# A list-scheduled attention and GeGLU kernel: partial-wave readiness in the scheduler, other pool sizes, one more full matmul asked for per three narrow waves, other POOL estimates, and a hold-off before tanh

## Chip, cores, metric

One core of one Trainium2 chip. The metric is device time in microseconds (us). Engines: PE (matmul), DVE (vector), ACT (activation), POOL (GpSimd), SP (issues DMAs).

## The reference, cut to what matters

```python
# x: [1, 2048, 512] bf16, 32 heads of 16
g = sigmoid((x * gate_w).sum(-1, keepdims=True))
q, k, v = split(x @ wqkv)
p = softmax(q @ k.T * 16**-0.5)          # per head, 2048 x 2048
a = (p @ v) @ wo
h = gelu_tanh(x @ w_gate) * (x @ w_up)   # 1376 columns
b = h @ w_down
return g * a + (1 - g) * b
```

## The kernel before

The kernel is written as about 7600 tasks. A list scheduler in Python gives each engine a fixed order, working from assumed durations; semaphores then enforce the true dependences. So an assumed duration never changes what an instruction costs. It only changes the order in which each engine's queue is laid down, and the chip runs these queues in order.

The attention is done in "waves" of matmuls on 32 rows. Pass A computes score tiles (128x512) and DVE takes their row maxima; pass B, 80 tiles later, recomputes the transposed tiles with the maximum subtracted, ACT takes exp, and PE multiplies with V ("PV"). A wide wave (D) has two A tiles and two B tiles, a narrow one (S) one of each. Four heads and 512 queries make a unit of 64 tiles; there are 32 units. Between the waves PE does the projections and the feed-forward half.

```python
# one unit, pass A done: its maxima go to PE by way of POOL  ("hand-over")
t_fin = add("dve", ..., name="fin%d" % u, ...)              # L1046 negm
t_hi  = add("pool", 260.0, ..., name="hi%d" % u, ...)       # L1056 CAST
t_lo  = add("pool", 270.0, ..., name="lo%d" % u, ...)       # L1060
#   then PE: QB = ident x QA + Msel x ident                 # L819, L1066
# one unit, PV done: row sums through DRAM, reciprocal, broadcast back
d4 = dma_task("n4_%d" % u, Rb..., 65536 * 4, ...)           # 256 KB, assumed 2.85 us
t_on[u] = add("pool", d_pool(512, 2.4), ..., deps=[d4, t_oe], ...)   # L1122, waits for d4
... # cut
# gelu of one 128x512 tile: ACT copy, three POOL ops, ACT tanh, two POOL ops, POOL times u
t_p3  = add("pool", ..., name="gp3_%d_%d" % (sc, fc), ...)  # L942
t_th2 = add("act", d_act(512) + 30.0, em, name="g_tanh%d_%d" % (sc, fc), deps=[t_p3], uses=[tm_tl])  # L948
... # cut
# dummies: full 128x128x512 matmuls on zeros ahead of a narrow wave, to hold PE's clock
if wna == 1 and plan is not None:
    ndum = plan.get(wi, 0)
# derive_plan, from a FIRST schedule without dummies: any 3 narrow waves in a row
# shall have plan_min full matmuls, at most dummy_max = 2 dummies each
have = sum(r[lo_:i_ + 1]) + sum(d[lo_:i_ + 1])
if have < want:
    d[i_] = min(C["dummy_max"], want - have)
```

## Time and profile before

| | before |
|---|---|
| time, median | 1444.74 us when predicted (4 runs), 1442.74 us over 16 runs |
| pass A (wide reduces) | 15.9 to 1369.9 us of the span |
| tail without reduces | 71.6 us |
| clock at half speed before the last reduce | 119.5 us in 9 stretches |
| full dummies (L1164) | 644 |

From the profile page of the kernel before: busy time of each engine, and the span in 40 slices with PE's granted clock in tenths.

```profile
span 1441.6 us, 22221 instructions
...
PE 1220.1 (85%) x8077; PEld 343.8 (24%) x8077; DVE 1262.8 (88%) x1449; ACT 1234.5 (86%) x2355; POOL 327.9 (23%) x386
...
PEclk9799999999989999998999998799999999799956
```

PE, DVE and ACT are almost equally busy. The 7s and 8s in the clock row are slices that hold stretches at half clock; the 56 at the end is the tail.

The costliest groups of before; columns: line, engine, op, shapes, count, busy us, mean ns, idle us just before and what ended it.

```profile
L1242 ACT ACTIVATE R<-ps 128x512 bf16<-128x512 f32 x2048 | 1098.5, 609 | 119.1 <-PE ps L1194 89.4
L1218 DVE TENSOR_REDUCE pmb<-ps 128x2 f32<-128x1024 f32 x683 | 835.5, 1223 | 87.7 <-PE ps L1194 75.9
...
L1225 DVE TENSOR_REDUCE pmb<-ps 128x1 f32<-128x512 f32 x682 | 463.9, 680 | 16.6 <-PE ps L1194 13.9
...
L1164 PE MATMUL ps<-wrm 128*128 128x512 bf16 x644 | 207.2, 399 | 50.3 <-PE ps L1194 23.2
```

Where DVE never waits, the timeline of before shows a wide and a narrow reduce every 1.81 us (start us, length us):

```profile
604.20 1.21 DVE L1218 TENSOR_REDUCE pmb<-ps 128x2 f32<-128x1024 f32 x1
...
605.37 0.69 DVE L1225 TENSOR_REDUCE pmb<-ps 128x1 f32<-128x512 f32 x1
...
606.00 1.23 DVE L1218 TENSOR_REDUCE pmb<-ps 128x2 f32<-128x1024 f32 x1
```

683 such pairs are 1236 us; pass A takes 1354 us. So about 100 us are lost where DVE waits for PE. Lines of the waits of before (who waited for whom: us, times, longest):

```profile
POOL R L1122 <- DMA Rb<-scr_li: 375.0, 30, 31.9
...
DVE pmb L1218 <- PE ps L1194: 75.9, 155, 2.8
...
POOL tmpb L954 <- ACT tmpb L948: 42.4, 40, 3.3
...
ACT tmpb L948 <- POOL tmpb L942: 4.3, 4, 2.3
```

The last line is four waits and 4.3 us in all.

### The profile page before, as it was taken

To read this page: it belongs to the slowest core of one execution; us is meant where nothing else is said; L and a number is where in the kernel's file an instruction comes from. 1 tells how busy PE (TensorE), PEld (TensorE's weight loads), DVE (VectorE), ACT (ScalarE), POOL (GpSimd) and SP (SyncE) were. 2 spreads that over 40 slices of the span, in tenths; PEclk is the share of its full clock that TensorE was granted. 3 is DMA by queue.
4 is the path that set the end of the run, shared out by engine and by line. 5 is a ranking of instruction groups with operands and counts; after the bars stand their busy time and mean duration, and the time that the engine had idled before them with its cause. 6 is when DMAs were issued, how large, how long until landed. Compare 5 with 4: busy or idle time off the path is not lost.

```text
span 1441.6 us, 22221 instructions
## 1 busy us (share of the span) xinstructions
PE 1220.1 (85%) x8077; PEld 343.8 (24%) x8077; DVE 1262.8 (88%) x1449; ACT 1234.5 (86%) x2355; POOL 327.9 (23%) x386
## 2 busy tenths in 40 slices
PE   9888888888888888889888888888888888888884
PEld 3322222222222222222222222222222222222211
DVE  8889889999987999998998998899998899899900
ACT  3189999999977999888998998799998998799991
POOL 2123431013323330013333410023332400000000
PEclk9799999999989999998999998799999999799956
DMA  6000000000000000000000000000000000000000
GB/s 220 1 15 9 10 2 9 8 10 9 9 9 15 9 9 9 9 9 9 1 9 23 9 9 9 2 9 8 9 9 20 12 9 1 8 9 9 9 8 23
DMA packets 23287, 21.11 MB, mean 15 GB/s; under 512 B 10928, under 2 KB 17424, under 8 KB 23184
## 3 DMA queue, kind: packets, MB, share of 16 engines
q1 hardware_dynamic: 23184, 19.70, 4.2%
q8 instruction: 69, 1.13, 0.3%
q14 instruction: 34, 0.28, 0.1%
HBM read 17.07 MB, written 2.62 MB: 14 GB/s over the span
## 4 chain that ended last, share of the span: by engine, by line
PE 45%; ACT 28%; DVE 20%; issue 4%; DMA 2%; POOL 1%; POOLq 0%
ACT R L1242 22%; PE ps L1177 19%; DVE pmb L1218 14%; PE ps L1164 8%; PE ps L1261 6%; DVE pmb L1225 6%; PE ps L819 5%; PE ps L1194 3%; PE ps L1298 2%; PE ps L992 2%; ACT tmpb L948 1%; DMA Rb<-scr_li 1%; ACT OSb L1099 1%; ACT KT L852 1%; ACT gbb L1002 1%
## 5 line engine op out<-in xcount | busy, mean ns | idle before, releaser
L1242 ACT ACTIVATE R<-ps 128x512 bf16<-128x512 f32 x2048 | 1098.5, 609 | 119.1 <-PE ps L1194 89.4
L1218 DVE TENSOR_REDUCE pmb<-ps 128x2 f32<-128x1024 f32 x683 | 835.5, 1223 | 87.7 <-PE ps L1194 75.9
L1177 PE MATMUL ps<-KT,QAb 32*128 32x512 bf16 x2048 | 540.8, 395 | 134.8 <-DVE pmb L1218 36.2
L1194 PE MATMUL ps<-QBb,KT 32*128 32x512 bf16 x2048 | 543.5, 405 | 6.2 <-PE ps L1261 3.2
L1225 DVE TENSOR_REDUCE pmb<-ps 128x1 f32<-128x512 f32 x682 | 463.9, 680 | 16.6 <-PE ps L1194 13.9
L1177 PEld LDWEIGHTS ps<-KT,QAb 32*128 32x128 bf16 x2048 | 138.8, 91 | 597.8 <-ACT R L1242 379.1
L1164 PE MATMUL ps<-wrm 128*128 128x512 bf16 x644 | 207.2, 399 | 50.3 <-PE ps L1194 23.2
L1261 PE MATMUL ps<-R,Vaug 128*17 128x512 bf16 x2048 | 209.6, 403 | 5.9 <-ACT R L1242 5.6
L1194 PEld LDWEIGHTS ps<-QBb,KT 32*128 32x128 bf16 x2048 | 126.8, 91 | 24.8 <-ACT R L1242 24.0
L1122 POOL TENSOR_TENSOR R<-OSb,Rb 128x512 bf16<-128x512 f32 x32 | 40.5, 1266 | 399.0 <-DMA Rb<-scr_li 375.0
L930 POOL TENSOR_TENSOR tmpb<-gsb 128x512 bf16<-128x512 bf16 (+1 forms) x44 | 45.7, 1038 | 237.6 <-ACT gsb L924 237.6
L1261 PEld LDWEIGHTS ps<-R,Vaug 128*17 128x17 bf16 x2048 | 49.2, 87 | 142.0 <-issue 103.4
L1164 PEld LDWEIGHTS ps<-wrm 128*128 128x128 bf16 x644 | 41.8, 97 | 144.3 <-ACT R L1242 134.8
L1056 POOL CAST Msel<-negm 128x16 bf16<-128x16 f32 x32 | 8.1, 252 | 297.9 <-DVE negm L1046 297.9
L976 POOL TENSOR_TENSOR gsb<-gsb,usb 128x512 bf16<-128x512 bf16 (+1 forms) x44 | 50.7, 1151 | 38.8 <-ACT usb L970 36.7
L819 PE MATMUL ps<-xT,wg 128*128 128x512 bf16 (+1 forms) x176 | 56.1, 388 | 0.8 <-ACT R L1242 0.6
L819 PE MATMUL ps<-xT,wu 128*128 128x512 bf16 (+1 forms) x176 | 55.1, 387 | 1.2 <-ACT R L1242 0.6
L1298 PE MATMUL ps<-R 128*128 128x512 bf16 x128 | 41.5, 452 | 16.5 <-POOL R L1122 13.6
L992 PE MATMUL ps<-wd,gsb 128*128 128x512 bf16 (+1 forms) x176 | 52.5, 383 | 0.0
L942 POOL TENSOR_TENSOR tmpb<-tmpb,gsb 128x512 bf16<-128x512 bf16 (+1 forms) x44 | 50.7, 1152 | 3.6
L960 POOL TENSOR_TENSOR gsb<-gsb,tmpb 128x512 bf16<-128x512 bf16 (+1 forms) x44 | 50.6, 1151 | 3.3
L1112 DVE RECIPROCAL Lci<-Lc 128x16 f32<-128x16 f32 x32 | 7.8, 244 | 46.3 <-DMA Lc<-scr_l 46.3
(62 smaller groups left out, 541.1 us busy)
## 6 DMA issues: line engine op xcount, KB each, us to landing
Rb<-scr_li SPq DMA_DIRECT2D x32, 256.0 KB
R<-in_A_x_dram SPq DMA_DIRECT2D x4, 512.0 KB, 6.4
out_dram<-R SPq DMA_DIRECT2D x16, 128.0 KB, 1.7
wg<-in_B_w_gate_dram SPq DMA_DIRECT2D x1, 1376.0 KB
wu<-in_B_w_up_dram SPq DMA_DIRECT2D x1, 1376.0 KB, 12.1
wd<-in_B_w_down_dram SPq DMA_DIRECT2D x1, 1280.0 KB, 14.5
R<-in_A_wqkv_dram SPq DMA_DIRECT2D x1, 1024.0 KB, 6.2
R<-in_A_wqkv_dram SPq DMA_DIRECT2D x1, 512.0 KB, 9.5
```

Of the source, the lines that this page charges most:

```text
L819: return [e.matmul(psum_ap(tl)[0:m, 0:n], lhsT=lhs_fn(c), rhs=rhs_fn(c), start=(c == 0), stop=(c == nmm - 1))]
L942: return [e.tensor_tensor(out=t_, in0=t_, in1=gsb[0:fr, gs_tl.slot, :], op=ALU.mult)]
L976: return [e.tensor_tensor(out=g_, in0=g_, in1=usb[0:fr, us_tl.slot, :], op=ALU.mult)]
L992: return [e.matmul(psum_ap(btl)[:, 0:D], lhsT=gsb[0:fr, gs_tl.slot, tt * 128:(tt + 1) * 128], rhs=wd[0:fr, fc, :], start=(fc == 0), stop=( ...
L1164: return e.matmul(psum_ap(atl)[:, 0:C["dummy_n"]], lhsT=wrm[:, 0:128], rhs=wrm[:, 0:C["dummy_n"]], start=True, stop=True)
L1177: return e.matmul(o, lhsT=QAb[32 * j:32 * j + 32, qt.slot, t * 128:(t + 1) * 128], rhs=KT[32 * j:32 * j + 32, g, kc * 512:(kc + 1) * 512], ...
L1194: return e.matmul(psum_ap(btl), lhsT=KT[32 * j:32 * j + 32, g, b * 128:(b + 1) * 128], rhs=QBb[32 * j:32 * j + 32, qt.slot, :], start=True ...
L1218: return [e.tensor_reduce(out=pmb[:, ids[0]:ids[0] + na], in_=i_, axis=AX.X, op=ALU.max)]
L1225: return [e.tensor_reduce(out=pmb[:, ids[0]:ids[0] + 1], in_=i_, axis=AX.X, op=ALU.max)]
L1242: return [e.activation(out=PTb[:, pt_tl.slot, :], in_=psum_ap(btl), func=ACT.Exp, scale=scale)]
L1261: return e.matmul(pv_ap[32 * jj:32 * jj + 17, :], lhsT=Vaug[:, bb, h, :], rhs=PTb[:, ptl.slot, :], start=(bb == 0), stop=(bb == NT - 1), t ...
L1298: return [e.matmul(psum_ap(atl)[:, 0:D], lhsT=ONb[:, ont.slot, tt * 128:(tt + 1) * 128], rhs=wo_pad[:, g, :], start=(g == 0), stop=(g == G ...
```

## The change

The intent is a scheduler that knows that a reduce may start when the A part of its wave is done, and settings tuned again on top of that. Six parts can change the order (the new place for dummies, `dummy_pos="D"`, is added but not used):

```diff
-    n_pt=12, n_os=3, n_on=9, n_gs=12, n_us=3, ...
+    n_pt=16, n_os=3, n_on=9, n_gs=11, n_us=3, ...
-    plan_win=3, plan_min=6,
+    plan_win=3, plan_min=7,
+    dummy_pos="S",
+    sl_tanh=2000.0,
...
         def d_pool(fd, rate=2.4):
-            return 60.0 + (rate * 0.87) * fd
+            if rate >= 2.0:
+                return 130.0 + 2.0 * fd
+            return 110.0 + 1.0 * fd
...
                     t_th2 = add("act", d_act(512) + 30.0, em, name="g_tanh%d_%d" % (sc, fc), ...,
-                                uses=[tm_tl])
+                                uses=[tm_tl], slackm=C["sl_tanh"])
...
                 for d in t.dependents:
+                    rt = t.done
+                    if t.idx in d.pdeps and t.cum is not None and t.xfer <= 0.0:
+                        rt = t.start + t.cum[d.pdeps[t.idx] - 1] + t.lat
...
-                    if t.done > d.est_ready:
-                        d.est_ready = t.done
+                    if rt > d.est_ready:
+                        d.est_ready = rt
... (cut: the event queue keyed per dependent, cum per wave, tail dummies of dummy_pos "D")
```

`slackm` makes the scheduler place a task only 2 us after it believes it to be ready. That is the "hold-off".

More of the change, by code (lines that the diff above doesn't have):

```diff
@@ L46 @@
         "dma_sem", "dma_val", "scheduled", "after", "table", "nafter_left", "succ_after",
-        "nunsched", "est_ready", "tight", "rel", "xfer", "wkind", "slackm", "ready_at", "pdeps",
+        "nunsched", "est_ready", "tight", "rel", "xfer", "wkind", "slackm", "ready_at", "pdeps", "cum",
     )
@@ L51, in __init__ @@
                  n_inst=1, lat=100.0, lock=None, boost=None, mode=None, banks=(), after=(), table=None, tight=False,
-                 rel=0.0, xfer=0.0, wkind=None, slackm=0.0, pdeps=()):
+                 rel=0.0, xfer=0.0, wkind=None, slackm=0.0, pdeps=(), cum=None):
         self.eng = eng
@@ L88, in __init__ @@
         self.ready_at = None
+        self.cum = cum
         self.pdeps = dict((d.idx, k) for (d, k) in pdeps)
@@ L346, in schedule @@
                 free_at[e] = t.end
-                events.append((t.done, t.idx, t))
+                events.append((t.done, t.idx, 0, t))
                 self.order[e].append(t)
@@ L354, in schedule @@
                 for d in t.dependents:
+                    rt = t.done
+                    if t.idx in d.pdeps and t.cum is not None and t.xfer <= 0.0:
+                        rt = t.start + t.cum[d.pdeps[t.idx] - 1] + t.lat
+                        if rt > t.done:
+                            rt = t.done
+                    events.append((rt, d.idx, 1, d))
                     d.nunsched -= 1
-                    if t.done > d.est_ready:
-                        d.est_ready = t.done
+                    if rt > d.est_ready:
+                        d.est_ready = rt
                     if d.nunsched == 0:
@@ L380, in schedule @@
             if events:
-                events.sort(key=lambda x: (x[0], x[1]))
+                events.sort(key=lambda x: (x[0], x[2], x[1]))
                 if nxt is None or events[0][0] < nxt:
@@ L396, in schedule @@
             while events and events[0][0] <= now + 1e-9:
-                _, _, t = events.pop(0)
-                n_done += 1
-                for tl in t.alloc + t.uses:
-                    tl.n_left -= 1
-                for d in t.dependents:
-                    d.ndeps_left -= 1
-                    if d.ndeps_left == 0 and d.nafter_left == 0:
-                        cand[d.eng].append(d)
+                _, _, kind, t = events.pop(0)
+                if kind == 0:
+                    n_done += 1
+                    for tl in t.alloc + t.uses:
+                        tl.n_left -= 1
+                else:
+                    t.ndeps_left -= 1
+                    if t.ndeps_left == 0 and t.nafter_left == 0:
+                        cand[t.eng].append(t)
         self.makespan = max(t.done for t in tasks) if tasks else 0.0
@@ L515 @@
 DEFAULT_CFG = dict(
-    n_pt=12, n_os=3, n_on=9, n_gs=12, n_us=3, n_gb=8, n_osb=3, n_qa=2, n_qb=2,
+    n_pt=16, n_os=3, n_on=9, n_gs=11, n_us=3, n_gb=8, n_osb=3, n_qa=2, n_qb=2,
     n_l=2, n_r=2, n_ms=2, n_tmp=3, n_ga=2,
@@ L536 @@
     qb_ident=True,
+    dummy_pos="S",
+    pvd_margin=8,
+    sl_tanh=2000.0,
     s_fd=512,
@@ L1141, in make_tasks @@
             first_pv = {}
+            first_pv_task = {}
             last_red = [None]
@@ L1159, in make_tasks @@
                     allocs.append(atl)
-                    if wna == 1 and plan is not None:
+                    if wna == 1 and plan is not None and C["dummy_pos"] == "S":
                         ndum = plan.get(wi, 0)
@@ L1198, in make_tasks @@
                     post.append(("B", m, ub, b, j, btl, ptt))
+                ntail = 0
+                pvu = None
+                if (a_ids and wna == 2 and plan is not None and C["dummy_pos"] == "D" and b_ids):
+                    ub0, ib0 = b_ids[0] // TPU, b_ids[0] % TPU
+                    ub1, ib1 = b_ids[-1] // TPU, b_ids[-1] % TPU
+                    if ub0 == ub1 and ib0 >= C["pvd_margin"] and ib1 < TPU - C["pvd_margin"] and ub0 in first_pv_task:
+                        ntail = plan.get(wi, 0)
+                        pvu = ub0
@@ L1200, in emw, with emz @@
+                for _d in range(ntail):
+                    def emz(e):
+                        return e.matmul(pv_ap[:, 0:C["dummy_n"]], lhsT=wrm[:, 0:128], rhs=wrm[:, 0:C["dummy_n"]],
+                                        start=False, stop=False, skip_group_check=True)
+                    parts.append(emz)
+                if ntail:
+                    deps.append(first_pv_task[pvu])
+                    deps.append(t_wrm0)
+                    uses.append(pv_tl[pvu])
                 def emw(e, parts=parts):
@@ L1201, in emw @@
                     return [p(e) for p in parts]
-                wdur = d_wave(len(parts) - ndum) + ndum * (C["dummy_n"] / 2.4 + 10.0) + (C["m_switch"] if ndum else 0.0)
+                nreal = len(parts) - ndum - ntail
+                dmy = C["dummy_n"] / 2.4 + 10.0
+                cum = []
+                tacc = 0.0
+                for k_ in range(ndum):
+                    tacc += dmy
+                    cum.append(tacc)
+                if ndum:
+                    tacc += C["m_switch"]
@@ L1203, in make_tasks @@
+                for k_ in range(nreal):
+                    tacc = (ndum * dmy + (C["m_switch"] if ndum else 0.0)) + d_wave(k_ + 1)
+                    cum.append(tacc)
+                if ntail:
+                    tacc += C["m_switch"]
+                for k_ in range(ntail):
+                    tacc += dmy
+                    cum.append(tacc)
+                wdur = tacc
                 tw = add("pe", wdur, emw, name="W%d" % wi, prio=prw, deps=deps, alloc=allocs, uses=uses,
                          n_inst=len(parts), mode="row", lat=C["m_wave_lat"], after=[prev_wave] if prev_wave is not None else [],
-                         tight=True, wkind=("D" if wna == 2 else "S") if a_ids else None)
+                         tight=True, wkind=("D" if wna == 2 else "S") if a_ids else None, cum=cum)
@@ L1206, in make_tasks @@
                 prev_wave = tw
                 wave_tasks.append((wi, wna, tw))
+                if ntail:
+                    pv_done[pvu].append(tw)
                 for it in post:
@@ L1242, in em @@
                             return [e.activation(out=PTb[:, pt_tl.slot, :], in_=psum_ap(btl), func=ACT.Exp, scale=scale)]
-                        t_ex = add("act", d_act(512), em, name="exp%d" % m, prio=prw + 0.0002,
-                                   deps=[tw], uses=[btl, pt_tl], table="exp", tight=C["exp_tight"])
+                        if C["part_dep"]:
+                            t_ex = add("act", d_act(512), em, name="exp%d" % m, prio=prw + 0.0002,
+                                       pdeps=[(tw, ndum + nreal)], uses=[btl, pt_tl], table="exp", tight=C["exp_tight"])
+                        else:
+                            t_ex = add("act", d_act(512), em, name="exp%d" % m, prio=prw + 0.0002,
+                                       deps=[tw], uses=[btl, pt_tl], table="exp", tight=C["exp_tight"])
                         pvq.append((m, ub_, b, j, t_ex, pt_tl))
@@ L1263, in make_tasks @@
                                 pparts.append(em)
+                            is_first_pv = ubb not in first_pv
                             if ubb not in first_pv:
@@ L1277, in make_tasks @@
                             pv_done[ubb].append(tpv)
+                            if is_first_pv:
+                                first_pv_task[ubb] = tpv
                             if (m % TPU) == TPU - 1:
@@ L1349, in derive_plan @@
                 pos[t.idx] = k
-            s_waves = [(wi, tw) for (wi, wna, tw) in wave_tasks if wna == 1]
+            key_na = 1 if C["dummy_pos"] == "S" else 2
+            k_waves = [(wi, tw) for (wi, wna, tw) in wave_tasks if wna == key_na]
             r = []
-            for n_, (wi, tw) in enumerate(s_waves):
+            for n_, (wi, tw) in enumerate(k_waves):
                 p0 = pos[tw.idx]
-                p1 = pos[s_waves[n_ + 1][1].idx] if n_ + 1 < len(s_waves) else len(order)
+                p1 = pos[k_waves[n_ + 1][1].idx] if n_ + 1 < len(k_waves) else len(order)
                 nfull = 0
@@ L1369, in derive_plan @@
             plan = {}
-            for i_, (wi, tw) in enumerate(s_waves):
+            for i_, (wi, tw) in enumerate(k_waves):
                 if d[i_] > 0:
```

## The prediction

> **What bounds it now.** From 15 to 1369 us runs a loop of 683 pairs of score waves (2 A tiles, then 1 A tile). The groups of instructions show DVE max-reduces of 1223 ns (128x1024) and 680 ns (128x512); in the timeline at 604-610 us, where DVE never waits, a pair takes 1.81 us. 683 pairs at 1.81 us are 1236 us, plus 16 us of small DVE work: about 1250 of 1354 us. So DVE is nearly the floor, and some 100 us are lost in stretches where PE or ACT is late: 76 us before the wide reduce wait for PE (waits). ACT (three exps in 1.57 to 1.61 us, plus 310 other activations) and PE are almost as full. Tail from 1369: 72 us, no reduces.
>
> **Clock.** The granted clock is 0.5 in nine stretches between 54 and 1242 us, 119 us in sum, each a multiple of 3.41 us (as the Trainium skill, "TensorE: Matmul & The Clock Gate", Part 1, describes: a window of 3413 ns, two states). Counting matmuls from the trace, the 3.4 us before each drop held 0 to 3 full 128x128x512 matmuls; most warm windows hold 4 to 6. The wide-and-narrow pair takes 2.48 us cold, 1.95 us warm on average: 119 us cold cost about 25 us. The dummies (L1164, x644) were planned on a schedule without them; in the trace 90 of 681 runs of three narrow waves hold under 6 full matmuls, against the plan's 6.
>
> **What the change does.**
> - plan_min 6 to 7: applying the plan's rule to the trace's order gives 631 dummies at 6 and 738 at 7. So about 100 more, at about 0.21 us each (two take 0.59 us, three 0.82): +21 us of PE, perhaps half on the path. It should remove a third to two thirds of the cold time: -8 to -17 us.
> - Partial readiness: actual reduce waits were already partial (their semaphore value); only the scheduler's estimate moves, by 25 or 50 ns per wave. Order shifts a little; exp still waits for the whole wave.
> - n_pt 12 to 16: exp can run four more tiles ahead of PV; fewer late exps and waves. PEld L1177 waits 379 us for exp, but mostly for PSUM banks, which stay at four. I give it -5 to -10 us.
> - sl_tanh 2 us: ACT waits for POOL before tanh only 4.3 us. At most -4 us.
> - d_pool closer to truth (1154 for 1151 measured; 622 for 617): order only. n_gs 12 to 11: about 0.
> - Tail: unchanged.
>
> **Sum:** -5 to -10 (clock less dummies, net small), -5 to -10 (pt), -2 to -8 (better-fitting order): about -20 us. Predicted 1423 us, 8 in 10 between 1397 and 1446. Faster by over 2%: 0.36; within 2%: 0.59; slower: 0.05.
>
> **What would show it.** L1164 count 720 to 770; cold time before 1369 us down to 40-80 us; mean durations of reduces and exps unchanged; DVE wait for PE before the wide reduce 76 to about 55-60 us; PE busy up or flat; last reduce at about 1350 instead of 1369; tail still about 72 us.
>
> **What would make it wrong.** The new order is a different list schedule, so cold stretches may fall elsewhere: if the plan and the final order disagree as before, cold time stays and only dummies are added (slower, 1450). If nearly all cold vanishes and pt slack lets DVE run at 1.81 us throughout, 1390 or less.

## The result

The median after is 1424.54 us (1418.63 to 1432.65, 11 runs) against 1442.74 us (16 runs). The ratio is 0.9877, 95% interval 0.9853 to 0.99: a clear gain of 1.2%, inside 2%. Ratios here compare the fast runs of the same rounds; they are not quite the ratio of the medians.

From the profile page of the kernel after:

```profile
span 1424.2 us, 22386 instructions
...
PE 1224.1 (86%) x8160; PEld 348.8 (24%) x8160; DVE 1261.7 (89%) x1449; ACT 1235.9 (87%) x2355; POOL 328.1 (23%) x386
...
PEclk9799999999999999899999999999989999899956
```

The groups of after that answer to those of before:

```profile
L1293 ACT ACTIVATE R<-ps 128x512 bf16<-128x512 f32 x2048 | 1100.3, 609 | 104.2 <-PE ps L1208 72.2
L1269 DVE TENSOR_REDUCE pmb<-ps 128x2 f32<-128x1024 f32 x683 | 835.6, 1223 | 77.8 <-PE ps L1208 67.6
...
L1276 DVE TENSOR_REDUCE pmb<-ps 128x1 f32<-128x512 f32 x682 | 463.5, 680 | 12.5 <-PE ps L1208 9.6
L1178 PE MATMUL ps<-wrm 128*128 128x512 bf16 x727 | 229.4, 390 | 63.7 <-PE ps L1208 35.9
```

And the waits of after; the line of a tanh waiting for POOL no longer exists; the opposite wait, of POOL for tanh, has grown from 42.4 to 92.4 us:

```profile
POOL R L1135 <- DMA Rb<-scr_li: 376.2, 32, 31.5
...
POOL tmpb L967 <- ACT tmpb L961: 92.4, 33, 5.5
...
DVE pmb L1269 <- PE ps L1208: 67.6, 144, 3.7
```

No instruction became faster: exp 609 ns, reduces 1223 and 680 ns, as before. The last wide reduce ends at 1354.2 us instead of 1369.9, and the tail is 69.9 us instead of 71.6. The trace's clock records show 71.7 us at half clock before the last reduce instead of 119.5. Wide reduces that start in warm time lose as much against 1.81 us a pair as before (85.4 us after, 86.1 before); those in cold time lose 17.5 us instead of 32.2. So between these two profiled runs the gain lies in the clock. That fits most of what I had said would show it. It does not say which part of the change brought it.

### The profile page after: what moved, and what is told of

Same layout as the page of the kernel before. It is cut to its first block, busy times and chain, and to the rows that moved or that the text cites. A ratio compares the mean times of both kernels' runs of the same rounds, so it can differ in the third digit from the quotient of the medians.

```text
span 1424.2 us, 22386 instructions
## 1 busy us (share of the span) xinstructions
PE 1224.1 (86%) x8160; PEld 348.8 (24%) x8160; DVE 1261.7 (89%) x1449; ACT 1235.9 (87%) x2355; POOL 328.1 (23%) x386
## 4 chain that ended last, share of the span: by engine, by line
PE 52%; ACT 25%; DVE 17%; issue 4%; DMA 1%; POOLq 0%; POOL 0%
PE ps L1191 21%; ACT R L1293 21%; DVE pmb L1269 12%; PE ps L1178 11%; PE ps L1316 6%; PE ps L832 6%; DVE pmb L1276 5%; PE ps L1208 4%; PE ps L1005 2%; PE ps L1356 1%; ACT OSb L1112 1%; ACT tmpb L961 1%; ACT usb L983 1%; ACT QBb L1104 1%; PE ps L740 1%
## 5 line engine op out<-in xcount | busy, mean ns | idle before, releaser
L1269 DVE TENSOR_REDUCE pmb<-ps 128x2 f32<-128x1024 f32 x683 | 835.6, 1223 | 77.8 <-PE ps L1208 67.6
L1178 PE MATMUL ps<-wrm 128*128 128x512 bf16 x727 | 229.4, 390 | 63.7 <-PE ps L1208 35.9
L1316 PE MATMUL ps<-R,Vaug 128*17 128x512 bf16 x2048 | 205.4, 397 | 1.1 <-ACT R L1293 0.8
L1178 PEld LDWEIGHTS ps<-wrm 128*128 128x128 bf16 x727 | 48.2, 96 | 170.4 <-ACT R L1293 155.7
L967 POOL TENSOR_SCALAR tmpb<-tmpb 128x512 bf16<-128x512 bf16 (+1 forms) x44 | 27.1, 617 | 92.4 <-ACT tmpb L961 92.4
```

The source lines that it names most:

```text
L1178: return e.matmul(psum_ap(atl)[:, 0:C["dummy_n"]], lhsT=wrm[:, 0:128], rhs=wrm[:, 0:C["dummy_n"]], start=True, stop=True)
L1269: return [e.tensor_reduce(out=pmb[:, ids[0]:ids[0] + na], in_=i_, axis=AX.X, op=ALU.max)]
L1316: return e.matmul(pv_ap[32 * jj:32 * jj + 17, :], lhsT=Vaug[:, bb, h, :], rhs=PTb[:, ptl.slot, :], start=(bb == 0), stop=(bb == NT - 1), t ...
```

## The experiments

Twelve kernels ran, five rounds each. The clock column is the mean granted clock over each kernel's fast runs. The wait column is DVE's wait for PE before the wide reduce in the profiled run. The before kernel's mean clock in these rounds was 0.9354 (43 runs).

| run | hold-off | plan_min | ratio to before | clock | wait, us |
|---|---|---|---|---|---|
| after | yes | 7 | 0.9877 | 0.957 | 67.6 |
| e1_plan7_alone | no | 7 | 0.9995 | 0.948 | 78.4 |
| e2_after_plan6 | yes | 6 | 0.9863 | 0.948 | 65.9 |
| e3_pt16_alone | no | 6 | 0.9982 | 0.934 | 79.3 |
| e4_after_old_ready | yes | 7 | 0.985 | 0.964 | 66.1 |
| e5_tanh_alone | yes | 6 | 0.9902 | 0.947 | 67.0 |
| e6_pool_alone | no | 6 | 0.9958 | 0.943 | 74.9 |
| null_n1 | no | 6 | 1.0137 | 0.922 | 88.5 |
| e7_after_no_tanh | no | 7 | 1.0034 | 0.947 | 82.1 |
| e9_move_tanh | moved by hand | 6 | 1.0169 | 0.920 | 107.6 |
| e10_replan6 | yes | 6, counted again | 0.9847 | 0.962 | 68.9 |
| e11_null_n1_tanh | yes | 6 | 0.9874 | 0.945 | 62.0 |
| e12_dma_for_holdoff | no, true DMA time | 7 | 0.988 | 0.965 | 69.8 |

### One part alone, one part undone

My theory at the start: the seventh full matmul in the plan keeps the clock up and brings the gain. The rival: the pools, or the scheduler's estimates.

e1_plan7_alone: `plan_min=6` to `plan_min=7` in the kernel before.

> The kernel before with plan_min 7 alone (730 dummies for 644). Clock theory: nearly the whole gain comes back, ratio to before 0.988 to 0.993 (1428 to 1433 us), cold time before the last reduce 60 to 85 us for 119. Rival (pools and the scheduler's estimates bring the gain): ratio 0.998 to 1.01, since 86 dummies at 0.21 us each only add up to 18 us of PE time.

Measured 0.9995 (0.9948 to 1.0042). The clock did rise, and the profiled run had 92 us at half clock for 119.5. But the time did not fall. **My theory failed here.**

e2_after_plan6: `plan_min=7` to `plan_min=6` in the kernel after.

> The kernel after with plan_min put back to 6 (638 dummies). Clock theory: the gain is lost, ratio to before 0.996 to 1.003 (1438 to 1447 us), cold time about 110 to 125 us again. Rival: ratio stays at 0.985 to 0.990.

Measured 0.9863 (0.9813 to 0.9913): the gain stays without the seventh matmul.

e3_pt16_alone: `n_pt=16, n_gs=11` in the kernel before.

> The kernel before with n_pt 16 and n_gs 11 alone. My prediction gave this part -5 to -10 us: ratio 0.993 to 0.9965. Clock theory: the plan is still 6, and this order has 12 runs of three narrow waves with 0 or 1 full matmul for 6 before, so cold time does not fall, and the ratio is 0.997 to 1.006. Rival (slack of the pools): 0.988 to 0.993.

Measured 0.9982 (0.9934 to 1.003): no gain to be seen; the interval still allows half a per cent.

e4_after_old_ready: `if t.idx in d.pdeps and ...:` to `if False:` in the kernel after, so that a wave again counts as ready only at its end.

> The kernel after, but the scheduler takes a wave as ready only at its end, as before; plan_min 7 and the pools stay (720 dummies). Clock theory: the estimate of readiness only reorders, so the gain stays, ratio to before 0.985 to 0.991, cold time 55 to 85 us. Rival (partial readiness is what pays): ratio 0.996 to 1.003.

Measured 0.985 (0.9805 to 0.9895): the part that gives the change its name is not what pays.

### The rest, and a null change

e5_tanh_alone: `slackm=2000.0` on the tanh task in the kernel before.

> The kernel before with the 2 us hold-off before tanh alone (643 dummies). After the first four runs my clock-by-plan_min theory has fallen, so the rest of the change is asked one part at a time. Theory T (the hold-off pays): ratio to before 0.984 to 0.991, mean granted clock 0.943 or more. Theory O (no single part pays; the gain is one order's share of cold stretches and waits): ratio 0.993 to 1.004. Direct effect of the hold-off on ACT's wait for POOL is 4 us at most, that is 0.997.

Measured 0.9902 (0.9848 to 0.9956).

e6_pool_alone: the new `d_pool` in the kernel before.

> The kernel before with the new estimate of POOL durations alone (637 dummies). Theory P (truer POOL durations pay): ratio to before 0.984 to 0.991. Theory O: 0.993 to 1.004. The truer durations move a tile's chain of POOL work by about 0.1 us only, so I expect O.

Measured 0.9958 (0.9911 to 1.0004): perhaps a little, not resolved.

null_n1: `m_wave_lat=130.0` to `131.0` in the kernel before, a change of one nanosecond in an assumed latency.

> A null change: the kernel before with the scheduler's wave latency 131 ns for 130, which should mean nothing, but reorders. It measures how much a mere other order moves the time. If orders differ little: ratio 0.997 to 1.003. If the order's chance decides (theory O): outside of that, and since this order has 11 runs of three narrow waves with 0 or 1 full matmul for 6 before, I expect it slower, 1.003 to 1.012, with mean clock 0.92 to 0.935.

Measured 1.0137 (1.0089 to 1.0184). A meaningless change moved the time by more than the change under study. Any single comparison of two orders has to be read against that.

e7_after_no_tanh: `sl_tanh=0.0` in the kernel after.

> The kernel after without the hold-off before tanh (720 dummies). Theory T: the gain is lost, ratio to before 0.997 to 1.003. Theory O: something between, 0.988 to 0.998, as the order differs again. If the hold-off does nothing at all: 0.985 to 0.990.

Measured 1.0034 (0.9993 to 1.0076): the whole gain is gone. This is what theory T asked for.

### What the hold-off covers

All kernels without the hold-off have a few tanh that make ACT wait. The timeline of the kernel before at 641 us shows one from its start to its end. ACT had delivered `gsb` for this tile at 639.50 us.

```profile
641.20 1.27 POOL L1122 TENSOR_TENSOR R<-OSb,Rb 128x512 bf16<-128x512 f32 x1 [23.94 <-ACT R L1242]
...
641.51 1.61 ACT L1242 ACTIVATE R<-ps 128x512 bf16<-128x512 f32 x3
...
642.43 1.04 POOL L930 TENSOR_TENSOR tmpb<-gsb 128x512 bf16<-128x512 bf16 x1
...
643.83 0.38 PE L1194 MATMUL ps<-QBb,KT 32*128 32x512 bf16 x1
644.25 1.15 POOL L942 TENSOR_TENSOR tmpb<-tmpb,gsb 128x512 bf16<-128x512 bf16 x1
644.29 0.68 DVE L1225 TENSOR_REDUCE pmb<-ps 128x1 f32<-128x512 f32 x1
645.43 0.63 ACT L948 ACTIVATE tmpb<-tmpb 128x512 bf16<-128x512 bf16 x1 [2.31 <-POOL tmpb L942]
...
646.60 0.39 PE L1261 MATMUL ps<-R,Vaug 128*17 128x512 bf16 x4 [2.38 <-ACT R L1242]
...
647.55 1.22 DVE L1218 TENSOR_REDUCE pmb<-ps 128x2 f32<-128x1024 f32 x1 [2.58 <-PE ps L1194]
...
648.29 0.60 PE L1177 MATMUL ps<-KT,QAb 32*128 32x512 bf16 x1
```

Read it downward. POOL stands in front of the multiply L1122, which needs the broadcast load `Rb`. (The bracket names ACT; but that releaser had long been done, and the other dependence is the DMA.) The gelu chain of a tile whose input was ready at 639.50 therefore starts at 642.43. Its tanh sits in ACT's queue in front of the next exps, so ACT waits 2.31 us, PE 2.38 us for an exp, DVE 2.58 us for PE. Then the clock drops at 648 us for 10.2 us: matmuls of 0.38 us take 0.60 us. That queues are in order is what the Trainium skill says ("TensorE: Matmul & The Clock Gate", the paragraph on engine queue depths, which calls ACT, DVE and each GpSimd core strict first-in first-out), and the 2.31 us here agree.

In the six kernels without the hold-off (before, e1, e3, e6, null_n1, e7), 18 tanh made ACT wait over 0.5 us. Just before each of the 18 POOL had been standing in front of L1122. Twelve of the 18 were followed within 4 us by a clock drop. In after, e2, e4 and e10 there is no such wait; in after every tanh starts at least 1.86 us after its POOL input is done. e5 has one left, of 0.75 us.

The load is late because the scheduler takes it to be faster than it is: 2.85 us from issue to use, while the trace of before shows a median of 4.86 us (4.68 to 5.18). For the tile above, SP's timeline has the issue 4.97 us ahead of the multiply:

```profile
636.23 0.55 SPq L737 DMA_DIRECT2D Rb<-scr_li  x1
```

The hold-off of 2 us covers just this error. Does its value come from that?

e9_move_tanh: the schedule of before kept, and only each tanh put three places later in ACT's queue.

```diff
         sch, mk, wave_tasks = make_tasks(plan)
+        acts = sch.order["act"]
+        for t in [t for t in acts if t.name.startswith("g_tanh")]:
+            k_ = acts.index(t)
+            acts.remove(t)
+            acts.insert(k_ + 3, t)
+            t.start = acts[k_ + 2].start + 0.001
```

> The kernel before with its schedule kept, PE's order the same instruction for instruction; only each of the 44 tanh is put three places later in ACT's order. In the trace of before four tanh made ACT wait for POOL (4.3 us), and the two longest (1.0 and 2.3 us, at 177 and 645 us) are each followed 3 us later by a clock drop (3.4 and 10.2 us). Theory S (a stalled in-order ACT starves PE, and the clock drops after it): no ACT wait before tanh, none of these two drops, ratio to before 0.990 to 0.996. Theory T in full (the hold-off is worth the 1 to 1.6 per cent seen so far by this direct path): 0.984 to 0.990. Theory O (only the reordering that the hold-off brings about counts): 0.997 to 1.003.

Measured 1.0169 (1.0123 to 1.0215): none of my three. The waits before tanh did go (one is left, 1.0 us, and a drop follows it), and the two drops with them. But the later tanh pushed POOL's second half of the chain into the hand-over. In the timeline of e9_move_tanh:

```profile
366.33 0.25 DVE L1046 TENSOR_REDUCE negm<-pmb 128x16 f32<-128x64 f32 x1
...
367.05 1.15 POOL L976 TENSOR_TENSOR gsb<-gsb,usb 128x512 bf16<-128x512 bf16 x1
...
368.14 0.25 POOL L1056 CAST Msel<-negm 128x16 bf16<-128x16 f32 x1
368.48 0.27 POOL L1060 TENSOR_TENSOR Msel<-negm,Msel 128x16 bf16<-128x16 f32 x1
...
368.84 0.58 PE L819 MATMUL ps<-QAb,ident 128*128 128x512 bf16 x1 [0.77 <-ACT R L1242]
...
370.03 1.22 DVE L1218 TENSOR_REDUCE pmb<-ps 128x2 f32<-128x1024 f32 x1 [1.56 <-PE ps L1194]
```

The maxima are ready at 366.58 us, the cast that PE needs starts at 368.14 behind the gelu multiply. Of the 32 hand-overs five let PE wait over 0.3 us here (6.1 us in all); in before none did. At half clock this profile spent 204.8 us before the last reduce; I have traced only some of the drops to this. What the run shows: this delay, which the other engines' orders didn't know about, moved stalls from one in-order queue to another. That this is the whole of the 1.7% is not shown.

e11_null_n1_tanh: the null change and the hold-off together.

> The null change (wave latency 131 ns) with the hold-off before tanh: does the hold-off help in a third family of orders? null_n1 stood at 1.0137. Theory T: at least 1 per cent lower than that, so 0.985 to 1.004. Theory O with no effect of the hold-off itself: anywhere between 0.995 and 1.015, so 1.005 or more speaks against T.

Measured 0.9874 (0.9825 to 0.9924), 2.6% below null_n1. So the hold-off lowers the time in all three families of orders in which I have it both ways: 1.0% (before), 1.6% (after, 0.9877 over 1.0034), 2.6% (the null order). With e12 below, the seven kernels whose plan has the hold-off or the true load lie at 0.985 to 0.990; the six whose plan has neither, before included, at 0.996 to 1.014 (e9, moved by hand, is left out). The two groups do not overlap, and that, more than any single pair, stands against the luck of the order.

e12_dma_for_holdoff: e7_after_no_tanh with the truth about the load in place of the hold-off.

```diff
+                d4.lat += 2000.0      # Rb load: 4.85 us instead of 2.85 us
-    sl_tanh=2000.0,
+    sl_tanh=0.0,
```

> The kernel of e7_after_no_tanh (the change without its hold-off, ratio 1.0034), with the truth about one transfer in its place: the scheduler takes the Rb load as 2 us longer (from 2.85 us to 4.85 us; the traces show 4.86 us median from its issue to the multiply that waits for it). In all 18 places where a tanh made ACT wait over 0.5 us, POOL had stood in front of that multiply just before. Theory D (the hold-off pays because it covers that late load): no ACT wait before a tanh over 0.5 us, no clock drop right after one, ratio 0.983 to 0.992, mean clock 0.952 or more, DVE's wait for PE before the wide reduce 70 us or less. Rival (the hold-off pays in another way): ratio 0.997 to 1.008 as in e7_after_no_tanh, with DVE's wait near 80 us, though the ACT waits are gone.

Measured 0.988 (0.985 to 0.9909), clock 0.965: as theory D asked on every point. The profiled run has no tanh wait over 0.12 us, and no clock drop next to one. DVE's waits in e7_after_no_tanh:

```profile
DVE pmb L1269 <- PE ps L1208: 82.1, 183, 2.9
...
ACT tmpb L961 <- POOL tmpb L955: 4.2, 4, 1.4
```

and in e12_dma_for_holdoff, where no line of a tanh waiting for POOL is left:

```profile
DVE pmb L1270 <- PE ps L1209: 69.8, 163, 2.7
```

### Dummies counted on the final order

The other kind of drop comes while the waves run, with few full matmuls between them. PE in the timeline of before:

```profile
885.33 1.04 PE L992 MATMUL ps<-wd,gsb 128*128 128x512 bf16 x4
886.30 0.39 PE L1177 MATMUL ps<-KT,QAb 32*128 32x512 bf16 x2
...
889.05 0.39 PE L1261 MATMUL ps<-R,Vaug 128*17 128x512 bf16 x4
...
890.54 1.01 PE L1164 MATMUL ps<-wrm 128*128 128x512 bf16 x2 [0.20 <-DVE pmb L1225]
891.48 0.60 PE L1177 MATMUL ps<-KT,QAb 32*128 32x512 bf16 x1
```

Between 886.37 and 890.54 us no full matmul starts; two narrow waves (at 886.93 and 888.73 us) have no dummy, though on this order the rule asks for two ahead of the second: it and the two narrow waves before it have only these four full matmuls. The clock drops at 890 us, and two dummies take 1.01 us instead of 0.59 us. The plan was made on an earlier schedule.

Are missing full matmuls what brings a drop? The traces with every matmul record in them (before, after, e9 to e12) say: only in part. From 36 us to the last wide reduce I cut them into the 3.41 us windows at whose edges every drop falls. Of the 2159 windows at full clock 49 end in a drop. None of the 1975 with less than 0.85 us of PE idle does; of the 29 with 1.25 us or more, 26 do. But of the 77 with no or one full matmul only 22 do. So lost PE time, added up over the window, tells the drops better than the plan's count. In the window before 890 us PE is idle for about 1.3 us, in short gaps; before the drop at 648 us, after the tanh wait, for about 2.3 us. (The ends of matmuls are modelled in these traces, so the limits are rough.)

e10_replan6 takes e2_after_plan6 and counts the dummies once more on the final order, without rescheduling:

```diff
         sch, mk, wave_tasks = make_tasks(plan)
+        plan = derive_plan(sch, wave_tasks)
+        # then add or remove dummies at the head of each narrow wave, and shift
+        # the semaphore counts of the tasks that wait for a part of it
```

> The kernel of e2_after_plan6 in the same order, but the dummies are counted once more on the final order and put where that order has fewer than 6 full matmuls in three narrow waves (628 for 638). Theory M (clock drops come from dummies planned for another order): mean clock 0.958 to 0.968 for 0.948, ratio to before 0.973 to 0.981, about 1405 to 1416 us. Rival (the drops come from stalls, not from the plan): clock 0.945 to 0.953, ratio 0.984 to 0.990 as in e2_after_plan6.

Measured 0.9847 (0.9801 to 0.9892), 1423.6 us. Theory M was right about the clock (0.962 for 0.948) and wrong about the time. By 0.014 of clock the time should have fallen by some 13 us (below); its mean fell by 2.9 us (1425.6 to 1422.7). My reading, which no run here tests, is that dummies put where the schedule had left no room for them cost what the clock gave; their number had even fallen, from 638 to 628. No kernel is clearly faster than after: the intervals of e2, e4 and e10 overlap with that of after.

### What the clock is worth

The 43 fast runs of the kernel before in these rounds are one program, and yet range from 1434 to 1456 us. Time and granted clock go together with a correlation of -0.97: 9.0 us for each 0.01 of mean clock. An 0.01 of a 1444 us span is 29 us at half clock, so a cold microsecond costs 0.31 us. With that number the dummies can be priced. e1 has 86 dummies more than before and 0.013 more clock, worth -11.6 us, yet its mean is 1.7 us above that of the 43 runs (0.3 us above before in its own rounds): the dummies cost about 13 us. after has 89 dummies more than e2 and 0.0095 more clock, worth -8.6 us, and is 1.1 us faster: they cost about 7.5 us. (These are estimates from means of 6 to 43 runs.)

The same price splits the gain of the hold-off. From before to e5 the mean falls by 13 us, of which the clock's rise in those rounds is worth 9; from e7 to after by 22, of which 9; from null_n1 to e11 by 34, of which 20; from e7 to e12, with the true load instead, by 20, of which 16. So the clock carries much of it, but not all. The profiled runs of e7 and after have the same 71.7 us at half clock before the last reduce; there the wide reduces in warm time lose 101.1 us in e7 and 85.4 us in after. That part is waiting, not clock.

## Why the prediction was right, and where not

The time was right: 1423 predicted, 1424.5 measured. So were most signs: 727 dummies (720 to 770 foreseen), 71.7 us cold (40 to 80), the last reduce at 1354 (about 1350), a tail of 70 (about 72), unchanged durations. DVE's wait fell to 67.6 us, where I had said 55 to 60. But the sum was right with wrong terms: that they added up to the measured gain is luck.

- "plan_min 6 to 7 ... +21 us of PE, perhaps half on the path ... -8 to -17 us." Both sizes hold: the clock gave 9 to 12 us, the dummies took 7.5 to 13 us. Their net was -1 us (after against e2) and +2 us (e1 against before). My sum entered it as "-5 to -10".
- "n_pt 12 to 16 ... -5 to -10 us." e3 shows nothing (0.9982, 0.9934 to 1.003).
- "Partial readiness: ... only the scheduler's estimate moves." Right; without it the ratio is 0.985.
- "d_pool ... order only." Measured 0.9958 alone, not resolved.
- "sl_tanh 2 us: ACT waits for POOL before tanh only 4.3 us. At most -4 us." **This is the step that failed.** Undoing it costs 1.6%, about 22 us; alone it brings 1.0%, about 14 us. I priced a wait by its own length. Two of those four waits were each followed by a clock drop, and the same late load that made them sat in every order's plan.
- "119 us cold cost about 25 us" was somewhat low: at 0.31 us each they cost 37 us.

What is shown: the gain hangs on the hold-off (e5, e7, e11), and naming the true duration of one DMA replaces it (e12, tried in one family of orders only). What is not: how all of the 14 to 22 us come about. The waits of before before a tanh (4.1 us over 0.5 us each) and the 13.6 us of drops that follow two of them (4.2 us at 0.31) make about 8 us. In after the remaining drops are fewer too, 47.8 us for 81.9 us without the first one at 54 us, and I can't say whether that belongs to the hold-off or to the luck of the order, with a null change worth 1.4%. I ran one null change only, so the spread of such luck is known only from how the two groups of kernels above scatter. n_pt and d_pool may matter together with the hold-off; that was not tried. Nor was a faster load instead of a truer estimate of it.

On the Trainium skill, as far as the argument rests on it: its clock page ("TensorE: Matmul & The Clock Gate", Part 1) describes a free-running window of 3413 ns and two states, and the trace agrees: every cold stretch in pass A of these kernels is a multiple of 3.41 us (3.4 to 31 us) at 0.5. Its DMA page ("DMA: Bandwidth & Descriptors", Anatomy of one DMA) fits 2.0 us plus bytes over 436 GB/s, from transfers issued by GpSimd; for 256 KB that would be 2.6 us, an estimate from that fit, close to the scheduler's 2.85. The trace has 4.86 us for this load, issued by SP, up to the start of its use; the measurement decides. Its packets say where the time goes: in before the first of 128 packets of 2 KB starts 1.34 us after the issue and the last ends 4.39 us after it (medians of the 32 loads), and between the two only 3.8 packets are in flight on average, on a core with 16 DMA engines.

## What to carry to other kernels

In a kernel with in-order queues laid down from assumed durations, look for the instruction whose assumption is furthest from the trace and that other work queues behind, and correct that number. A margin on a later task stood in for it here where the scheduler knew the margin (e5, e7, e11), and made things worse where it did not (e9). Price a wait by what queues behind it, here two more engines and PE's clock, not by its own length. And before crediting a part of a change, run a null change of the order and both "alone" and "all but": here the named part did nothing, and one nanosecond moved 1.4%.

## What the Trainium skill lacked or had wrong

- "TensorE: Matmul & The Clock Gate", in its closing table, ties drops to single PE-idle gaps of over about 3 us; Part 1 also tells of a mode in which PE "micro-idles" often enough, without a figure. Here the clock drops while PE runs: in e10 at 1001 us with 0.87 us of idle in the 3.41 us before and no gap over 0.26 us, in before at 890 us with about 1.3 us of idle and no gap over 0.50 us. The page has no limit for idle time added up over a window; in six traces no window under 0.85 us dropped, and 26 of 29 with 1.25 us or more did.
- "DMA: Bandwidth & Descriptors" has a fit for loads issued by GpSimd and none for SP. For this 256 KB broadcast load from DRAM it gives 2.6 us, an estimate, and the runs show 4.86 us to first use with 3.8 packets in flight on average. The page does have a rule for how many engines a transfer is spread over; I did not try it on this load.
- No page that I found warns how a wait in one in-order queue passes on to others: 2.31 us on ACT became 2.38 us on PE and 2.58 us on DVE, and a clock drop of 10.2 us followed.
